# Two layers of cached attention and feed-forward: order of key loads, places of rolled loops, and spare products at the layer border

## The chip, the core and the metric

The kernel runs on one core of one Trainium2 chip. The metric is device time in microseconds (us), the median of several runs. A run's time is a little longer than the span of its instructions in the profile. The engines are TensorE (PE, with its weight loads as PEld), VectorE (DVE), ScalarE (ACT), GpSimd (POOL) and SyncE (SP). SP issues every load here.

## The reference

One step of decoding for a batch of 4, through an attention block, a feed-forward block, and then both once more with the same weights and the same caches. A "layer" below is one pass through attention and feed-forward.

```
attention(x):  q = x @ wq                     # 512 -> 32 heads of 128
               scores = q . k * 128 ** -0.5   # 8 key heads, 4 query heads each, 8192 keys
               o = softmax(scores) @ v
               return concat(o) @ wo
ffn(x):        return (silu(x @ w_gate) * (x @ w_up)) @ w_down      # 512 -> 1792 -> 512
x = x + attention(layernorm(x));  x = x + ffn(layernorm(x))
x = x + attention(layernorm(x));  x = x + ffn(layernorm(x))
```

All inputs are bfloat16. The key and value caches are 4 x 8 x 8192 x 128 each, 64 MB of keys and 64 MB of values, and both layers read them; 273 MB come from memory in one execution.

## The kernel before

**Units.** The work of a layer is cut into 32 units, one for each pair of key head and batch row. A unit has a key block K and a value block V of 2 MB each. Eight slots of 2 MB on the chip hold such blocks (`NSLOT`, tile `kvf`). Layer 0 takes the units in order, 0 to 31. Layer 1 begins with units whose blocks are still on the chip (`kept`), then takes the rest. In this text K29 or V27 is the block of the unit at place 29 or 27 of its layer's order (`unit_order[L]`).

**Order of compute.** `work(L)` (line 320) gives the order in which blocks are computed: K(i), then V(i-1), and so on, with the end K28, V27, K29, V28, K30, K31, V29, V30, V31. `keys` and `values` (542, 568) write the operations of a block out. A key block has eight parts. For each, DVE transposes the keys in place (`turn`, tile `kvf`), and four products on PE add its scores to a bank (`scores`, output `ps<-kvf,zq`). Then a short chain makes the softmax: DVE takes the row maximum (`max_p`, `one<-ps`), PE transposes it and DVE reduces it (`max_t`, `m<-ps`), ACT copies it (`pb<-m`), PE spreads it, ACT scales it (`exps`, `one<-ps,rstd`) and takes the exponentials, DVE transposes the probabilities (`turn_p`, `pT<-pb`), and PE sums them (`total`). A value block is 16 products of 512 columns (`ps<-kvf,pT`), after which ACT and DVE pick out each head's own rows (`own_first`, `own_others`, `acc<-ps,own`). After every fourth unit `out_proj` (648) multiplies with `wo` (`o<-ps`, `ps<-o,wo_sb`). The last two value blocks of a layer use a form with small products (`block_last`, `ps<-pT,kvf`).

**Order of loads.** The list `items` (329) is the order in which SP issues loads. It is the compute order, without the kept blocks, followed by the feed-forward weights of the layer. `pump` issues the next item when its slot is free and stops at the first one whose slot is not. `home` (347) gives each block its slot. In program order a slot is free when its last block is finished; on the chip SP waits on a semaphore for it. SP's queue is in order, so an issue that waits holds back all behind it. The weights of the feed-forward block use slots 6 and 7.

**The layer border.** `center` and `deviation` (675, 693) make the layer norm: DVE sums, a product with ones on PE, and DVE again. `ffn` (743) runs `gate` and `up` (4 x 14 products each, weights `kvf` or, for a part kept from layer 0, `wq_sb`), a chain on DVE and ACT that makes hT, and 14 x 4 products with `w_down` (`ps<-scr,kvf`). While layer 0's `ffn` runs, it already frees places and issues parts of the first keys of layer 1 (`part`). `keep_up3` (727) copies a piece of `w_up` to another place and issues the last of these parts; the copy waits for PE's last read of `wq`. The first two key blocks of layer 1 then hand their slots on in quarters (`quarter`).

**Products that nobody reads.** `warm(n)` (669) makes n products of 128 x 128 with 256 columns from `wq_sb` into the score bank `SBK[1]`. Nothing reads them. Before the change five are made, all at the start of layer 1 (`center(L)`, `warm(L)`, `qrows(..., L)`).

**Rolled loops.** The operations of PE, DVE and ACT are first written to tapes. `roll` (796) finds a stretch of each layer that repeats every four units (`CYCLE`) and plays it as a loop. Where a unit begins on an engine's tape is noted in `heads`; for all three engines this happens in `keys`, when the first block of scores is written (line 546). The loop is opened with

```
with nc.Fori(1, 1 + turns, 1, engines=(only,), head_slot={only: 0}) as i:
```

`head_slot` is the place, counted in instructions, in a block of fetched code at which the loop's first instruction is put; the code ahead of the loop ends with a branch to it. Each product takes two instructions on PE, a weight load and the product.

Of the kernel before, what the change touches and what calls it, by code (L numbers as in the profile page):

```python
# [145 lines left out]
def bass_interleave_layers__gqa_block_cached__swiglu_ffn__decode_kernel(  # L146
# [20 lines left out]
    KT = D // P  # L167
# [16 lines left out]
    NV = NB // 2  # L184
    RUN = 1 << 15
    WIDE = 32
    assert TB == 2 * NA and NV * REP <= QB
    NU = B * G
    scale = float(Dh) ** -0.5
# [2 lines left out]
    with ExitStack() as es:  # L192
# [52 lines left out]
        n = 2 * FO * B  # L245
# [34 lines left out]
        T = _Sync(nc, engines, prog)  # L280
# [48 lines left out]
        items = []  # L329
        for L in range(2):  # L330
            seq = [it for it in work(L) if it not in kept]
            items += seq + [("wg",)] + [("wu",)] * (L == 0) + [("wd",)]
        for n, it in ((3, ("wo", 0)), (6, ("wo", 1)), (9, ("wo", 2)), (12, ("wo", 3))):
            items.insert(n, it)
# [165 lines left out]
        def max_t(u):  # L500
            T.pe(bank(STEP)[0:1, 0:P], mx[:], identf[:], reads=["mx", "ident"], writes=[f"pb{STEP}"],
                 is_transpose=True, start=True, stop=True)
            T.op("dve", lambda e: e.tensor_reduce(m4[:], bank(STEP)[0:1, 0:P].rearrange("p (x h) -> p h x", h=REP),
                                                  AX.X, ALU.max, negate=True),
                 reads=[f"pb{STEP}"], writes=["m4"])
            T.op("act", lambda e: e.activation(mrow.rearrange("p (x h) -> p x h", h=REP),
                                               m4[:].unsqueeze(1).to_broadcast([1, QB, REP]), ACTF.Copy),
                 reads=["m4"], writes=["pb"])
# [33 lines left out]
        def keys(L, u):  # L542
            def block(q):
                first = u == unit_order[L][0]
                if q == 0:
                    for n in T.LATE:
                        heads[n].append(len(T.tape[n]))
                if q == 0 and not first:
                    place_q(u)
                scores(L, u, q)  # L550
                if q == 0 and first:
                    deviation(lsc_sb, "lsc")
                if ("K", L, u) in heirs and (q + 1) % (NB // NQ) == 0 and q < NB - 1:
                    quarter(("K", L, u), q // (NB // NQ))
                if q == NB - 1:
                    finished(("K", L, u))
                    for gap, fn in ((0.0, max_p), (1.0, max_t), (0.9, exps), (1.0, turn_p), (0.3, total)):
                        line.append([gap, u, lambda fn=fn: fn(u)])

            i = unit_order[L].index(u)  # L560
            ahead = unit_order[1][i + 2] if L == 1 and i in (1, 2) else u
            for q in range(NB):
                if (L, ahead, q) not in turned:
                    turn(L, ahead, q)
                blocks.append((0.65, lambda q=q: block(q)))
                drain(LAG)
# [176 lines left out]
        def ffn(last):  # L743
            gb, ub = OBK
            gT = bank(gb)[:, 0:FO * B]
            uT = bank(ub)[:, 0:FO * B]
            fb = lambda ap: ap.rearrange("p (f b) -> p f b", b=B)
            rb = rstd[:].unsqueeze(1).to_broadcast([P, FO, B])
            ks = items[ends[0] + 1:ends[0] + 3]
            n = NB // NQ  # L750
            w6 = KT * F // (TB * Dh) // n * n
            for (w_sb, wname, bk) in (([wg_sb[:, k, :] for k in range(KT)], "wg", gb), (wu_sb, "wu", ub)):
                out = bank(bk)[:, 0:WIDE // B * FO * B].rearrange("p (r f b) -> p f r b", f=FO, b=B)
                for kt in range(KT):
                    if bk == gb and kt == KT // 2:
                        deviation(zero_sb, "zero")
                    for fo in range(FO):
                        f = fo // 2 * 2 * P + fo % 2
                        w = up3(f) if bk == ub and kt == FR and last else w_sb[kt][:, f:f + 2 * P - 1:2]
                        T.pe(out[:, fo, :, :], w, few(xn[:, kt * B:(kt + 1) * B]),  # L760
                             start=(kt + fo == 0), stop=(kt == KT - 1 and fo == FO - 1),
                             reads=["up3"] if bk == ub and kt == FR and last else at_w[wname] + [f"{wname}{kt}", "xn"],
                             writes=[f"pb{bk}"],
                             sig=(fo == FO - 1 and kt == KT - 1))
                if bk == gb and not last:
                    place(ks[0], NKEEP)
                    part(ks[0], NKEEP, 0, w6, sem_p[0])
            T.op("dve", lambda e: e.tensor_tensor(fb(gr), fb(gT), rb, ALU.mult),
                 reads=[f"pb{gb}", "rstd"], writes=["gr"])
            T.op("act", lambda e: e.activation(eg, gr, ACTF.Exp, scale=-1.0), reads=["gr"], writes=["eg"])  # L770
            T.op("dve", lambda e: e.tensor_tensor(fb(gw), fb(gr), rb, ALU.mult), reads=["gr", "rstd"], writes=["gw"])
            T.op("dve", lambda e: e.tensor_scalar(eg, eg, 1.0, None, op0=ALU.add), reads=["eg"], writes=["eg"])
            T.op("dve", lambda e: e.reciprocal(eg, eg), reads=["eg"], writes=["eg"])
            T.op("dve", lambda e: e.tensor_tensor(eg, gw, eg, ALU.mult), reads=["gw", "eg"], writes=["eg"])
            T.op("dve", lambda e: e.tensor_tensor(hT, eg, uT, ALU.mult), reads=[f"pb{ub}", "eg"], writes=["hT"])
            out = bank(OUTB)[:, 0:WIDE // B * XB].rearrange("p (r n b) -> p n r b", n=KT, b=B)
            for fo in range(FO):
                for nt in range(KT):
                    T.pe(out[:, nt, :, :], wd_sb[:, fo, nt * P:(nt + 1) * P], few(hT[:, fo * B:(fo + 1) * B]),
                         start=(fo + nt == 0), stop=(fo == FO - 1 and nt == KT - 1),  # L780
                         reads=["hT"] + at_w["wd", fo // 2], writes=[f"pb{OUTB}"], sig=(nt == KT - 1 and fo % 2 == 1))
                if not last and (f1 - f0 + (fo + 1) * D) % (n * TB * Dh) == 0:
                    i = (f1 - f0 + (fo + 1) * D) // (n * TB * Dh) - NQ
                    if i == 0:
                        part(ks[0], NKEEP, w6, NB, sem_p[1])
                        place(ks[1], NKEEP + 1)
                    else:
                        part(ks[1], NKEEP + 1, (i - 1) * n, i * n, sem_p[1 + i])
            if last:
                T.op("dve", lambda e: e.tensor_tensor(xn[:], xT[:], bank(OUTB)[:, 0:XB], ALU.add),  # L790
                     reads=["x", f"pb{OUTB}"], writes=["xn"])
            else:
                add_to_x()


        def roll(name):
# [18 lines left out]
            for L in range(2):  # L815
                run = {}
                for n in range(L * NU + 1, L * NU + NU - CYCLE - 1):
                    m = n
                    while m + CYCLE < L * NU + NU - 1 and said[m] == said[m + CYCLE] and strides(m) and \
                            strides(m) == strides(n + (m - n) % CYCLE):  # L820
                        m += 1
                    run[n] = m - n
                n = max(run, key=run.get)
                turns = run[n] // CYCLE + 1
                assert turns >= 3
                step = {}
                for k in range(n, n + CYCLE):
                    for key, d in strides(k).items():
                        assert step.setdefault(key, d) == d
                assert step.get(None, 1) == 1  # L830
                T.play(name, ops[at:heads[name][n]])
                with nc.Fori(1, 1 + turns, 1, engines=(only,), head_slot={only: 0}) as i:
                    for k in range(n, n + CYCLE):
                        value = {}
                        for _, _, left, _, _ in part[k]:
                            for sem_, v in left:
                                d = step[id(sem_)]
                                value[id(sem_), v] = engine.to_reg(i * d + (v - d))  # L838
                        T.play(name, part[k], lambda sem_, v: value[id(sem_), v], lambda g: i + (g - 1))
                at = heads[name][n + CYCLE * turns]  # L840
# [13 lines left out]
        for L in range(2):  # L854
# [26 lines left out]
            drain(0.0)  # L881
            flush(line)
            flush(after)
            center()
            ffn(L == 1)

        ob = bank_bf(LNB)
# [38 lines left out]
```

## Time and profile before

| | |
|---|---|
| median of 3 runs | 648.72 us (647.23 to 649.49) |
| the profiled execution, its own time | 649.32 us |
| its span | 647.5 us |
| mean granted clock of TensorE | 0.847 |
| busy: PE, DVE, ACT | 511.1, 446.1, 118.2 us |
| bytes read | 273.42 MB, 422 GB/s over the span |

How to read the rows shown in the prediction. A row of the stretches has the window, its length, the busy time and number of instructions of PE, PEld, DVE, ACT and POOL, the share of its clock that TensorE was granted (1.00 is full), the share of time that the transfer engines were busy, and GB/s. A row of the time order has the start in us, the time it took, engine, line, operation, output and inputs, shapes and the number of instructions merged; in brackets stands how long the engine was idle before it and what it waited for. There "issue" means that the engine waited for nothing that the profile shows. A row of the chain of waits has start, length, what ran, and how many. Since helpers record every operation, nearly all rows have line 99 (PE), 117 (the other engines) or 135 (loads); the tiles tell them apart.

### The profile page before, as it was taken

The numbers are of one execution on the slowest core, as the hardware profiler recorded it, in microseconds if no ns is written. First come the engines' busy times: TensorE is split into PE (matmuls) and PEld (weight loads), VectorE is DVE, ScalarE is ACT, GpSimd is POOL, SyncE is SP. The second block draws the span as 40 slices with busy tenths as digits, with TensorE's granted clock in tenths as the row PEclk, the third lists the DMA queues.
The fourth block names the chain that finished last, engine by engine and source line by source line (L and its number), as shares of the span: only waits on it lengthen the run. The fifth ranks groups of instructions, "written<-read, shape, count | busy, mean of one in ns | idle before, by whom it ended". The sixth has DMA issues, their size and how long they took to land.

```text
span 647.5 us, 12443 instructions
## 1 busy us (share of the span) xinstructions
PE 511.1 (79%) x4901; PEld 328.9 (51%) x4901; DVE 446.1 (69%) x1075; ACT 118.2 (18%) x393; POOL 19.3 (3%) x73
## 2 busy tenths in 40 slices
PE   1757887878878787888887986888888778787886
PEld 1534554545445554554555663555554455454556
DVE  2556576776876767776763745979796777678683
ACT  0011121211221211221221212222121222122121
POOL 0000000000000000000000000000000000000000
PEclk9998687787977879787796997989797978879795
DMA  8999999999999999999999999999999999999995
GB/s 357 434 432 423 431 441 423 437 437 421 442 433 423 441 431 427 442 427 427 441 412 413 393 439 413 417 433 433 427 439 431 427 443 427 431 439 427 424 431 244
DMA packets 12750, 273.83 MB, mean 423 GB/s; under 512 B 3048, under 2 KB 3056, under 8 KB 3056
## 3 DMA queue, kind: packets, MB, share of 16 engines
q1 hardware_dynamic: 12720, 273.44, 98.7%
q8 instruction: 18, 0.29, 0.2%
q14 instruction: 12, 0.10, 0.0%
HBM read 273.42 MB, written 0.00 MB: 422 GB/s over the span
## 4 chain that ended last, share of the span: by engine, by line
DMA 48%; PE 24%; DVE 23%; issue 3%; ACT 1%; SPq 0%; DVEq 0%; POOL 0%; ACTq 0%; POOLq 0%
DMA kvf<-in_A_k_cache_dram 48%; PE ps L99 24%; DVE kvf L117 14%; DVE acc L117 4%; DVE pT L117 1%; DVE one L117 1%; DVE m L117 1%; ACT pb L117 0%; SPq L135 0%; DVE scr L117 0%; ACT acc L117 0%; DVE oT L117 0%; DVEq L838 0%; DVE o L117 0%; DVE xn L117 0%
## 5 line engine op out<-in xcount | busy, mean ns | idle before, releaser
L117 DVE STREAM_TRANSPOSE kvf<-kvf 128x512 f32<-128x512 f32 x488 | 322.3, 686 | 72.2 <-DMA kvf<-in_A_k_cache_dram 72.2
L99 PE MATMUL ps<-kvf,zq 128*128 128x256 bf16 x2048 | 334.6, 308 | 19.1 <-DVE kvf L117 12.0
L99 PEld LDWEIGHTS ps<-kvf,zq 128*128 128x128 bf16 x2048 | 205.7, 112 | 89.9 <-DVE kvf L117 35.7
L117 ACT ACTIVATE pb<-m 1x128 f32<-1x128 f32 x64 | 19.7, 308 | 439.7 <-DVE m L117 439.7
L99 PE MATMUL ps<-kvf,pT 128*16 128x512 bf16 x960 | 69.8, 415 | 2.0 <-DVE rl L117 2.0
L117 DVE SCALAR_TENSOR_TENSOR acc<-ps,own,acc 128x128 f32<-128x128 f32 x180 | 63.1, 351 | 7.4 <-ACT acc L117 2.7
L117 DVE TENSOR_REDUCE one<-ps 128x1 f32<-128x256 f32 x64 | 25.8, 404 | 34.9 <-PE ps L99 34.5
L99 PE MATMUL ps<-identf,one 128*1 128x128 f32 x64 | 18.0, 282 | 39.2 <-DVE one L117 39.0
L99 PE MATMUL ps<-head,acc 128*128 128x4 f32 x120 | 24.7, 276 | 20.1 <-DVE acc L117 19.9
L99 PEld LDWEIGHTS ps<-identf,one 128*1 128x1 f32 x64 | 5.2, 80 | 69.2 <-DVE one L117 62.3
L99 PEld LDWEIGHTS ps<-head,acc 128*128 128x128 f32 x120 | 20.5, 214 | 36.4 <-DVE acc L117 35.3
L99 PEld LDWEIGHTS ps<-kvf,pT 128*16 128x16 bf16 x960 | 19.4, 92 | 35.6 <-issue 24.6
L99 PE MATMUL ps<-o,wo_sb 128*128 128x32 bf16 x256 | 26.8, 186 | 13.2 <-DVE o L117 13.2
L117 ACT ACTIVATE pb<-ps,one,rstd 128x256 bf16<-128x256 f32 x64 | 36.0, 563 | 2.1
L482 POOL TENSOR_TENSOR zq<-scr,quad 128x64 bf16<-128x64 bf16 x62 | 18.1, 292 | 603.5 <-PE ps L99 564.3
L99 PE MATMUL ps<-one,pb 1*128 1x1 f32 x128 | 26.4, 273 | 11.3 <-ACT pb L117 11.2
L99 PEld LDWEIGHTS ps<-one,pb 1*128 1x128 f32 x128 | 21.0, 204 | 28.3 <-ACT pb L117 24.9
L117 DVE STREAM_TRANSPOSE pT<-pb 128x256 bf16<-128x256 bf16 x64 | 26.0, 407 | 8.0 <-ACT pb L117 7.9
L99 PEld LDWEIGHTS ps<-o,wo_sb 128*128 (+1 forms) x256 | 22.7, 103 | 16.9 <-issue 9.3
L99 PEld LDWEIGHTS ps<-rsm,one 128*128 128x128 f32 x128 | 24.5, 237 | 8.3 <-ACT rsm L117 6.4
L99 PE MATMUL ps<-rsm,one 128*128 128x4 f32 x128 | 21.9, 242 | 5.2 <-ACT rsm L117 5.2
L117 DVE TENSOR_TENSOR xT<-xT,ps 128x16 f32<-128x16 f32 x17 | 2.9, 171 | 31.5 <-PE ps L99 31.5
(64 smaller groups left out, 202.2 us busy)
## 6 DMA issues: line engine op xcount, KB each, us to landing
kvf<-in_A_k_cache_dram SPq DMA_DIRECT2D x56, 2048.0 KB, 29.0
kvf<-in_A_v_cache_dram SPq DMA_DIRECT2D x56, 2048.0 KB, 32.6
kvf<-in_A_k_cache_dram SPq DMA_DIRECT2D x20, 512.0 KB, 7.4
kvf<-in_A_v_cache_dram SPq DMA_DIRECT2D x20, 512.0 KB, 10.8
wq_sb<-in_A_wq_dram SPq DMA_DIRECT2D x4, 1024.0 KB, 7.7
wo_sb<-in_A_wo_dram SPq DMA_DIRECT2D x8, 512.0 KB, 37.8
kvf<-in_B_w_gate_dram SPq DMA_DIRECT2D x8, 448.0 KB, 15.8
kvf<-in_B_w_down_dram SPq DMA_DIRECT2D x14, 256.0 KB, 16.9
```

The lines of the kernel that those rows point to most:

```text
L99: return e.matmul(out, lhsT=lhsT if at is None else lhsT(place(at)), rhs=rhs, **kw)
L117: self.tape[engname].append((repr((name, args, kw)), lambda e, _: getattr(e, name)(*args, **kw), left, sig, None))
L482: T.op(eng, lambda e: e.tensor_tensor(dst, q4, m4_, ALU.mult), reads=keys_ + ["quad"], writes=["zq"])
```

## The change

Five edits, in three groups.

```diff
         for L in range(2):
             seq = [it for it in work(L) if it not in kept]
+            for k, v in ((29, 27), (30, 28)):
+
+                it = ("K", L, unit_order[L][k])
+                seq.remove(it)
+                seq.insert(seq.index(("V", L, unit_order[L][v])), it)
             items += seq + [("wg",)] + [("wu",)] * (L == 0) + [("wd",)]
```

The end of each layer's list of loads was K28, V27, K29, V28, K30, K31, V29, V30, V31. It becomes K28, K29, V27, K30, V28, K31, V29, V30, V31. The order of compute stays.

```diff
+    HEADS = (0, 100)
...
-                    for n in T.LATE:
+                    for n in ("pe", "dve"):
                         heads[n].append(len(T.tape[n]))
...
+            heads["act"].append(len(T.tape["act"]))
             T.op("act", lambda e: e.activation(mrow.rearrange("p (x h) -> p x h", h=REP),
...
-                with nc.Fori(1, 1 + turns, 1, engines=(only,), head_slot={only: 0}) as i:
+                with nc.Fori(1, 1 + turns, 1, engines=(only,), head_slot={only: HEADS[L] if name == "pe" else 0}) as i:
```

ACT's units now begin at the copy of the maximum in `max_t`, so its loops begin there too. PE's loop in layer 1 is put at slot 100 instead of 0; in layer 0 it stays at 0.

```diff
+                    if bk == ub and kt == KT - 1 and not last:
+                        warm(1)
                     for fo in range(FO):
...
             for fo in range(FO):
+                if not last:
+                    warm(1 + (fo == 0) if fo % 2 == 0 else 0)
                 for nt in range(KT):
...
-            center()
+            center(1 - L)
             ffn(L == 1)
```

At the border between the layers twelve products more are made that nobody reads: in `center` after layer 0's attention two before the product with ones and one behind it; in layer 0's `up` one ahead of the last 14 products; in layer 0's `w_down` loop two before the first group of four products and one before every second group after it (six). Layer 1's end gets none.

## The prediction

> **What bounds the kernel now.** I read the page's slices and chain first, then the stretches where the transfers fall off, then what each engine waited for there, and last the time order of the two layer ends.
>
> ```profile
> DMA  8999999999999999999999999999999999999995
> DMA 48%; PE 24%; DVE 23%; issue 3%; ACT 1%; SPq 0%; DVEq 0%; POOL 0%; ACTq 0%; POOLq 0%
> 500.00:600.00 100.00, 79.48 (x652) 48.51 (x647) 75.09 (x176) 19.47 (x66) 3.22 (x11) 0.88 1.00 433
> 350.00:355.00 5.00, 4.74 (x50) 3.20 (x51) 3.04 (x10) 2.33 (x4) 0.00 (x0) 0.50 1.00 406
> 355.00:360.00 5.00, 4.50 (x31) 3.21 (x29) 1.26 (x3) 0.02 (x1) 0.29 (x1) 0.75 0.96 334
> 360.00:365.00 5.00, 5.00 (x51) 3.33 (x49) 4.69 (x11) 1.52 (x5) 0.29 (x1) 1.00 0.98 397
> 395.00:400.00 5.00, 3.55 (x32) 2.73 (x33) 2.08 (x6) 1.12 (x4) 0.00 (x0) 0.50 0.97 411
> 400.00:405.00 5.00, 4.55 (x39) 2.28 (x37) 3.99 (x9) 1.77 (x6) 0.29 (x1) 0.82 0.96 393
> 405.00:410.00 5.00, 4.70 (x48) 2.77 (x45) 4.95 (x13) 0.08 (x1) 0.29 (x1) 1.00 1.00 406
> 640.00:645.00 5.00, 3.96 (x135) 3.66 (x132) 1.73 (x7) 0.63 (x3) 0.00 (x0) 0.50 0.19 77
> ```
>
> The transfers fill nearly every slice, at 433 GB/s where nothing disturbs them (500 to 600 us). So time is to be had in three places only. **Border**, 350 to 365 us: 406, 334 and 397 instead of 433, (27 + 99 + 36) x 5 / 433 = 1.9 us lost. **Dip**, 395 to 410 us: (22 + 40 + 27) x 5 / 433 = 1.0 us. **Tail**: transfers fade after 640 us and the span lasts to 647.5. A wait anywhere else is covered by loads already queued.
>
> The sum is made against the profiled execution, 649.32 us (span 647.5 and 1.82 around it). It lies 0.6 above the median of 648.72, so I take the change in us from the one and put it on the other. A measurement of this kernel can tell about 0.3% (1.9 us) from no change.
>
> **ScalarE's loop starts elsewhere.** The head of its repeated block moves from the first score block of a unit to the copy of the maximum in `max_t`.
>
> ```profile
> ACT one L117 <- issue: 11.4, 2, 5.9
> 46.09 0.26 ACT L117 ACTIVATE one<-ps,rstd 128x1 f32<-128x1 f32 x1 [5.88 <-issue]
> 36.07 37.20 DMA kvf<-in_A_k_cache_dram
> 388.84 0.31 ACT L117 ACTIVATE pb<-m 1x128 f32<-1x128 f32 x1 [5.25 <-DVE m L117]
> 394.91 0.26 ACT L117 ACTIVATE one<-ps,rstd 128x1 f32<-128x1 f32 x1 [5.51 <-issue]
> 396.45 0.61 PE L99 MATMUL ps<-o,wo_sb 128*128 128x32 bf16 x16 [4.17 <-DVE o L117]
> 400.81 0.47 SPq L135 DMA_DIRECT2D kvf<-in_A_k_cache_dram  x1
> ```
>
> Twice, once for each layer, ScalarE stood 5.9 and 5.5 us with nothing to wait for, between two steps of one softmax: its instructions were not there. Behind it in layer 1 waited exp, DVE's turn of the probabilities, the cast of o, PE (4.17 us), and so the keys' load at 400.81: that is the dip. In layer 0 the load issued at 36.07 landed 37 us later, so the queue was deep and that stall cost nothing. The edit removes no instruction; the fetch now comes ahead of the copy of the maximum, which waits 5.25 us for DVE anyway. Of 5.51 that leaves 0.3 bare. Value -1.0, the whole dip, since keys that load 5 us sooner outrun a loss of 1.0; ends 0 (the loads come no sooner) and -1.0.
>
> **Keys before values.** For the units 29 and 30 of each layer's order K is issued before V27 and V28; SP issues the same loads, none added. Each moves past one load of 2 MB, 2.1 / 433 = 4.85 us.
>
> ```profile
> 564.84 0.47 SPq L135 DMA_DIRECT2D kvf<-in_A_v_cache_dram  x1
> 577.61 0.47 SPq L135 DMA_DIRECT2D kvf<-in_A_k_cache_dram  x1
> 577.61 26.55 DMA kvf<-in_A_k_cache_dram
> 603.51 1.04 PE L99 MATMUL ps<-kvf,pT 128*16 128x512 bf16 x16
> 605.26 0.27 PE L99 MATMUL ps<-identf,one 128*1 128x128 f32 x1 [0.71 <-DVE one L117]
> 604.18 0.71 DVE L117 STREAM_TRANSPOSE kvf<-kvf 128x512 f32<-128x512 f32 x1 [2.71 <-DMA kvf<-in_A_k_cache_dram]
> 606.34 0.24 DVE L117 TENSOR_REDUCE m<-ps 1x4 f32<-1x128 f32 x1
> 610.72 5.59 PE ps L99 x34
> ```
>
> On SP, K29 waits until 577.61 for its slot, and V27 (issued at 564.84) now queues behind it, 13 us later. That starves nothing: a load issued at 577.61 lands 26.55 later, so some 26 us, less the 4.85 of V27, are ahead of it. K29 lands at 599.3 and V27 at 604.2, the places exchanged. DVE then need not stand 2.71 us for K29: its first transpose and the maximum of the unit before run early. But PE's V27 products, at 603.51 now, wait until 604.2 (0.7), and the maximum's transpose stands behind them at 605.3, as before. DVE reads it at 605.5 instead of 606.34, because its two queued key transposes are done. So the late one becomes V27, and the gain is 0.8 and not 4.85. From 610.72 to the end PE and DVE hand on to each other without waiting for a load, so it is carried. Value -0.7; ends 0 (V27 waits a whole load) and -1.6 (the floor below). At the end of layer 0 the same gain runs into the border.
>
> **PE's block in layer 1 starts at slot 100.** Both programs' loops hold the same instructions; what moves is where PE's code crosses from one fetched block to the next after the loop: 100 slots sooner, 50 products (a load and a product each).
>
> ```profile
> 633.56 1.86 PE ps L99 x64
> 638.47 3.44 PE ps L99 x109
> 641.91 0.47 issue
> 642.38 0.31 PE ps L99 x5
> 642.99 1.69 PE ps L99 x56
> kvf<-in_B_w_down_dram SPq DMA_DIRECT2D x2, 256.0 KB, 16.8
> 625.39 3.39 SPq L135 DMA_DIRECT2D kvf<-in_B_w_down_dram  x2
> ```
>
> PE stops 0.47 us at 641.91, five products short of the end of `up`. That crossing moves to 55 products short, 50 x 3.44 / 109 = 1.6 us sooner; the crossing before it also moves 50 products, 50 x 1.86 / 64 = 1.5 us sooner, and with it the fetch. So fetch and need move together, and the 0.47 may go. Value -0.4; ends -0.5 (gone) and +1.1 (the fetch comes no sooner: it ends at 642.38 and 50 products still follow). **Floor:** the last of `w_down`, issued some 0.6 after 625.39, lands 16.8 later, at 642.8; the last eight products behind it (8/56 x 1.69 = 0.2) end at 643.1, where 644.7 stands now. The tail can give 1.6, and I take 1.1 of it.
>
> The Trainium skill ("Runtime: NRT & Kernel Launch", section "Instruction fetch mechanics") calls the crossing of a block mostly hidden. By that this term is nil and the sum 0.4 smaller; the 0.47 here, and the 2.93 below, speak against it.
>
> **Products that nobody reads.** `center` of layer 0 gets 3, `up` 1, `w_down` 8: twelve, on PE alone.
>
> ```profile
> 342.94 12.09 SPq L135 DMA_DIRECT2D kvf<-in_A_k_cache_dram  x8
> 347.17 0.29 PE L99 MATMUL ps<-xn,kvf 128*128 128x32 bf16 x5 [2.93 <-issue]
> 347.77 1.67 PE L99 MATMUL ps<-scr,kvf 128*128 128x32 bf16 x56 [0.31 <-DVE scr L117]
> 349.28 0.59 PE L99 MATMUL ps<-wq_sb 128*128 128x256 bf16 x2
> L99 PE MATMUL ps<-wq_sb 128*128 128x256 bf16 x5 | 1.7, 388 | 0.0
> 352.46 6.25 PE ps L99 x34
> 384.59 2.38 PE L99 MATMUL ps<-kvf,zq 128*128 128x256 bf16 x20
> 347.20:350.60 3.40, 3.04 (x66) 2.31 (x65) 0.61 (x4) 0.00 (x0) 0.00 (x0) 0.51 1.02 422
> ```
>
> Two that exist take 0.59 together and one 0.39, so 0.2 is added by each. The 3 and the 1 and the first 2 of `w_down` stand before waits of 0.3 to 0.5 us (for DVE's sums, the `up` weights, hT): hidden. The other 6, 1.2 us, lie between `w_down` products that PE now runs without a stop, since the 2.93 us at the fetch has let the weights land. Nothing in the change shortens that fetch: its crossing only moves four products forward. Behind PE wait SP's loads into the places that `w_down` frees, and the first keys' scores of layer 1. Those scores run at half clock now (6.25 us for 34, 184 ns; 119 ns at full), and a fuller stretch from 347.2 could lift it. The 0.7 from the earlier keys and 32 x 0.065 = 2.1 from a raised clock stand against 1.2 of products. The border's transfers cannot give more than 1.9. Value 0, between -1.9 (the stop vanishes too, or the clock rises) and +4.7 (12 x 0.388, all in the way).
>
> The Trainium skill ("TensorE: Matmul & The Clock Gate", section "What's actually happening") has the clock rise after one busy window of about 3.4 us. By that the filled stretch would lift it before the scores, and the sum would be 1.9 larger: the first rival. That 3.04 of 3.40 us busy were not enough here leaves it open.
>
> **Sum:** -1.0 - 0.7 - 0.4 + 0 = -2.1, 647.2 for the profiled execution, 646.6 for the median.
>
> **Rivals.** (1) *The border gains too.* The products hold the clock, the first scores end 2 us sooner, and SP refills before the queue runs dry: -2.1 - 1.9 = -4.0, 644.7. For it: 334 GB/s in 355:360 with PE busy at half clock. Against: the 2.93 us stop, which these products do not touch. Chance 0.22.
> (2) *Only the end moves.* The dip stays because ScalarE's fetch, wherever it stands, is not covered (5.25 us of wait against 5.51, and PE's half clock behind it), and the border takes what layer 0 gained: -1.1, 647.6. For it: the transfers fill all slices. Against: the load at 400.81 hangs on that very stall. Chance 0.25.
> (3) *Slower: the products stand in the way.* Place: the `w_down` loop of layer 0. It decides if they run after the weights have landed and the clock stays low: then up to 12 x 0.388 = 4.7 us come ahead of the first keys' scores, and SP's loads start as much later, in a stretch whose queue is already near empty. 4.7 - 2.1 = +2.6, 651.3. For it: the fetch stop, which makes PE the late one. Against: half of the twelve have a wait to lie in. Chance 0.12.
> (4) *No effect of the reordering* as V27 is waited for instead, and the fetch in the tail lands in a worse place (+1.1): about -1.0 + 1.1 = 0, 648.8. Chance 0.06.
> The forecast has 0.35.
>
> **Numbers.** Forecast 646.6, its own range +-0.9 from the two tail terms. Faster by over 0.3% (under 646.8) are (1) and some 0.28 of the forecast's 0.35: 0.50. Within are (2), (4) and the forecast's rest: 0.38. Slower: (3), 0.12. The range goes from a little under (1), 644.2, to 649.6, between (4) and (3).
>
> **What would show it.** ScalarE: no 5.5 us "issue" row near 390, PE's 4.17 for o gone, 433 GB/s in 400:410. Keys: DVE's 2.71 near 604 gone, out_proj's products some 0.7 sooner against the transfers. Slot 100: no "issue" row in `up` of layer 1. Border: the 2.93 row still there, the products of `w_down` taking 2.9 instead of 1.7 us, and the GB/s of 355:365 telling (1) from (3). The forecast is wrong if the dip stays, or if transfers in 350:365 fall well below 334.

## The result and the profile after
| | before | after |
|---|---|---|
| median | 649.01 us (647.23 to 651.4, 20 runs) | 647.11 us (646.37 to 648.24, 20 runs) |
| the profiled execution, its own time | 649.32 us | 646.91 us |
| its span | 647.5 us | 645.1 us |
| mean granted clock of TensorE | 0.847 | 0.862 |

The ratio of after to before is 0.9967, with a 95% interval of 0.9959 to 0.9975: 0.33% faster, some 2.1 us, where 2.1 had been forecast (647.2 for the profiled execution).

The stretches of the kernel after, with the columns of the prediction's rows (window, length, busy time of PE, PEld, DVE, ACT and POOL, granted clock, share of the transfers, GB/s):

```profile
350.00:355.00 5.00, 4.40 (x51) 2.97 (x51) 3.25 (x12) 2.16 (x4) 0.00 (x0) 0.66 0.98 416
355.00:360.00 5.00, 4.50 (x40) 3.46 (x39) 2.43 (x6) 0.50 (x2) 0.29 (x1) 1.00 0.91 331
360.00:365.00 5.00, 4.82 (x48) 3.15 (x47) 4.72 (x11) 1.75 (x6) 0.29 (x1) 1.00 1.00 406
395.00:400.00 5.00, 5.00 (x35) 2.45 (x34) 2.80 (x7) 0.07 (x1) 0.29 (x1) 0.58 0.98 419
400.00:405.00 5.00, 4.24 (x35) 2.80 (x32) 4.85 (x12) 1.70 (x6) 0.00 (x0) 1.00 1.03 437
405.00:410.00 5.00, 4.34 (x45) 2.74 (x43) 4.88 (x13) 1.77 (x6) 0.29 (x1) 1.00 1.01 434
640.00:645.00 5.00, 2.41 (x75) 2.01 (x71) 1.22 (x5) 0.00 (x0) 0.00 (x0) 0.84 0.11 43
```

The dip is gone: 419, 437 and 434 GB/s stand where 411, 393 and 406 stood. The border is as it was: 416, 331 and 406 against 406, 334 and 397. The tail has shrunk.

At the dip, first ACT's row in the table of waits (us in total, times, longest), then ACT's and PE's rows in time order around layer 1's loop head:

```profile
ACT pb L117 <- issue: 5.7, 1, 5.7
```

```profile
389.29 0.31 ACT L117 ACTIVATE pb<-m 1x128 f32<-1x128 f32 x1 [6.86 <-DVE m L117]
389.50 0.34 ACT L117 ACTIVATE acc<-ps,own 128x128 f32<-128x128 f32 x1
390.06 0.26 ACT L117 ACTIVATE one<-ps,rstd 128x1 f32<-128x1 f32 x1 [0.22 <-PE ps L99]
393.32 0.61 PE L99 MATMUL ps<-o,wo_sb 128*128 128x32 bf16 x16 [0.58 <-DVE o L117]
```

One such stop is left, layer 0's. In layer 1 the copy of the maximum now begins the loop; ACT waits 6.86 us for DVE there anyway, and whatever the fetch takes lies inside that wait. The scaling follows the copy by 0.77 us (389.29 to 390.06), not by 6.07 (388.84 to 394.91), and PE waits 0.58 us for o instead of 4.17.

The late loads, in time order (SP's issue of V27, then PE and DVE):

```profile
577.69 0.59 SPq L135 DMA_DIRECT2D kvf<-in_A_v_cache_dram  x1
603.98 1.04 PE L99 MATMUL ps<-kvf,pT 128*16 128x512 bf16 x16 [0.40 <-DMA kvf<-in_A_v_cache_dram]
605.25 0.28 DVE L117 TENSOR_REDUCE m<-ps 1x4 f32<-1x128 f32 x1
```

V27 has become the late block, as forecast: it lands 26.2 us after its issue, at 603.9 (604.2 forecast). From the landing to DVE's maximum it is now 605.25 - 603.9 = 1.3 us; before, from K29's landing at 604.16 (577.61 + 26.55), it was 606.34 - 604.16 = 2.2. In the traces of the experiments below it is 2.2 wherever the order of loads is the old one (five traces, with before) and 1.3 to 1.5 wherever it is the new one (nine, with this).

The chain of waits in the tail, and then the end of `up` in time order:

```profile
609.68 5.16 PE ps L99 x34
...
632.08 1.77 PE ps L99 x64
...
640.84 1.63 PE ps L99 x56
```

```profile
639.87 0.54 PE L99 MATMUL ps<-xn,wq_sb 128*128 128x32 bf16 x14
```

No row of "issue" splits the 14 products of `up`, where 9 and 5 stood around 0.47 us. The 2.4 us of span, set against the rows of before, divide into four: up to 609.68 1.04 (stream and keys), from there to 632.08 0.44 (the 34 products took 5.16 instead of 5.59, at a granted clock of 0.67 instead of 0.50), to 640.84 0.67 (the stop of 0.47 among it), and 0.25 behind, most of it the clock too.

The border, in time order and then from the chain:

```profile
344.60 0.56 PE L99 MATMUL ps<-xn,kvf 128*128 128x32 bf16 x14 [0.30 <-DMA kvf<-in_B_w_up_dram]
...
348.94 0.36 PE L99 MATMUL ps<-scr,kvf 128*128 128x32 bf16 x8 [0.69 <-DMA kvf<-in_B_w_down_dram]
```

```profile
335.15 14.29 DMA kvf<-in_B_w_down_dram
...
349.48 0.38 PE ps L99 x8
...
352.62 4.92 PE ps L99 x34
```

This is not what was forecast. The 2.93 us stop is gone, the landings of `w_down` pace the products (the last at 335.15 + 14.29 = 349.44), and the spare products lie in those waits. The last eight products end at 349.86, 0.40 later than before (347.77 + 1.67 = 349.44), and the first scores of layer 1 begin at 352.62 instead of 352.46: the border as a whole stayed where it was.

### The profile page after: what moved, and what is told of

The parts are those of the page before. It is cut to its first block, busy times and chain, and to the rows that moved or that the text cites. A ratio compares the mean times of both kernels' runs of the same rounds, so it can differ in the third digit from the quotient of the medians.

```text
span 645.1 us, 12463 instructions
## 1 busy us (share of the span) xinstructions
PE 509.1 (79%) x4913; PEld 327.5 (51%) x4913; DVE 445.6 (69%) x1075; ACT 118.3 (18%) x393; POOL 19.3 (3%) x73
## 4 chain that ended last, share of the span: by engine, by line
DMA 53%; DVE 21%; PE 21%; SPq 3%; issue 2%; ACT 1%; DVEq 0%; POOL 0%; POOLq 0%
DMA kvf<-in_A_k_cache_dram 47%; PE ps L99 21%; DVE kvf L117 13%; DMA kvf<-in_A_v_cache_dram 4%; DVE acc L117 4%; SPq L135 3%; DMA kvf<-in_B_w_down_dram 2%; DVE one L117 1%; DVE pT L117 1%; DVE m L117 1%; DVE scr L117 0%; ACT pb L117 0%; DVEq L849 0%; DVE oT L117 0%; ACT acc L117 0%
## 5 line engine op out<-in xcount | busy, mean ns | idle before, releaser
L99 PE MATMUL ps<-kvf,pT 128*16 128x512 bf16 x960 | 67.1, 402 | 2.0 <-DVE rl L117 1.2
```

Source lines behind the costliest of these rows:

```text
L99: return e.matmul(out, lhsT=lhsT if at is None else lhsT(place(at)), rhs=rhs, **kw)
```

## The experiments
Two theories stood at the start. **A**: three of the parts (ScalarE's loop head, keys, slot) each take a piece, and the spare products do nothing. **B**: the spare products do part of it, since the border's stop is gone where they run. The first four kernels are the kernel before with one part alone, the next four the whole change with one part left out.

**Keys alone.**
```diff
+            for k, v in ((29, 27), (30, 28)):
+                it = ("K", L, unit_order[L][k])
+                seq.remove(it)
+                seq.insert(seq.index(("V", L, unit_order[L][v])), it)
```


> The kernel before with the new order of loads alone. Theory A (each of three edits gives its own share, in its own place): K29 lands some 4.85 us before V27, the first transpose of K29 no longer waits 2.7 us, the products of wo that follow come about 0.7 us sooner against the loads, and the time falls by 0.7 to 1.1 us (0.11 to 0.17%). The 5.5 us issue row of ScalarE in layer 1 and the 393 GB/s of 400 to 405 us stay. Theory B (the gain is the border's: the spare products remove PE's 2.93 us stop at the fetch): no gain here, within 0.3 us.

Ratio 0.9990 (0.9977 to 1.0003). **ScalarE's loop head alone.**
```diff
-                    for n in T.LATE:
+                    for n in ("pe", "dve"):
...
+            heads["act"].append(len(T.tape["act"]))
```


> The kernel before with ScalarE's loop head moved alone. Theory A: the 5.5 us issue row in layer 1 goes into the wait for DVE's maximum, the stretch 400 to 405 us has over 425 GB/s, and the time falls by 0.5 to 1.0 us. Theory B: no gain, within 0.3 us; the loads are covered anyway. The issue row of layer 0 stays 5 to 6 us long in both.

Ratio 0.9990 (0.9981 to 0.9999). **Slot 100 alone.**
```diff
+    HEADS = (0, 100)
...
+                with nc.Fori(1, 1 + turns, 1, engines=(only,), head_slot={only: HEADS[L] if name == "pe" else 0}) as i:
```


> The kernel before with PE's loop of layer 1 at slot 100 alone. Theory A: no issue row in up of layer 1 (0.47 before), the end 0.4 to 0.6 us sooner. Theory B: no change, within 0.3 us. A third way: the fetch lands in a worse place, and the time grows by up to 1.1 us.

Ratio 0.9992 (0.9983 to 1.0002). **The spare products alone.**
```diff
+                    if bk == ub and kt == KT - 1 and not last:
+                        warm(1)
...
+                if not last:
+                    warm(1 + (fo == 0) if fo % 2 == 0 else 0)
...
-            center()
+            center(1 - L)
```


> The kernel before with the twelve products alone. Theory A: within 0.4 us of before, on either side; what PE gains at the fetch, if anything, the last weights of w_down take back. Theory B: the 2.93 us issue row at the border is gone or under 1 us, the loads in 350 to 365 us recover, and the time falls by 1 to 2 us. The slower rival of the prediction: the products stand in the way and the time grows by over 1 us.

Ratio 1.0005 (0.9993 to 1.0017). Each of the first three gives about 0.1%, too little to tell from nothing in two of the three; the products give nothing. The next four leave one part of the whole change out.

**Without the spare products.**
```diff
-                    if bk == ub and kt == KT - 1 and not last:
-                        warm(1)
...
-                if not last:
-                    warm(1 + (fo == 0) if fo % 2 == 0 else 0)
...
-            center(1 - L)
+            center()
```


> The changed kernel without the twelve products: keys, ScalarE's loop head and slot 100 together. Theory A (three shares that add, the products worth nothing): a ratio of 0.996 to 0.998 to before, as the whole change has (0.9967), no 5.5 us row of ScalarE in layer 1. Theory B (the products carry the gain): 0.999 to 1.000. A third way, from the products alone, which measured 1.0005: they cost a little, and this is the fastest of all, 0.996 or under.

Ratio 0.9969 (0.9957 to 0.9982), which is that of the whole change. In its time order the stop at the border is back, and costs nothing:

```profile
345.98 0.29 PE L99 MATMUL ps<-xn,kvf 128*128 128x32 bf16 x5 [1.70 <-issue]
346.58 1.46 PE L99 MATMUL ps<-scr,kvf 128*128 128x32 bf16 x48 [0.31 <-DVE scr L117]
349.20 0.40 PE L99 MATMUL ps<-scr,kvf 128*128 128x32 bf16 x8 [1.16 <-DMA kvf<-in_B_w_down_dram]
```

PE stands 1.70 us for nothing that the profile shows, catches up with 48 products, and then waits 1.16 us for the last landing: the end is at 349.60, 0.26 before that of the whole change. Theory B falls.

**Without the earlier keys.**
```diff
-            for k, v in ((29, 27), (30, 28)):
...
-                seq.insert(seq.index(("V", L, unit_order[L][v])), it)
```


> The changed kernel with the old order of loads. Theory A: K29's first transpose waits 2.7 us again near 604, and the time is 0.5 to 1.0 us longer than with the whole change, a ratio of 0.9975 to 0.9985. Rival (the keys' share is the noise of its own run): 0.9967 stays.

Ratio 0.9989 (0.9979 to 0.9998). Here the stop at the border was long in the profiled execution, as its time order and the chain show:

```profile
346.45 0.40 PE L99 MATMUL ps<-xn,kvf 128*128 128x32 bf16 x9 [2.21 <-issue]
```

```profile
346.45 3.67 PE ps L99 x73
```

The 73 products are 9 of `up`, the 56 of `w_down` and 8 spare ones, run without a wait to 350.12. The last weights, issued at 334.9, had landed 13.3 us later, at 348.3. So behind a long stop the spare products do stand in the way: without them the last eight, some 0.4 behind that landing, could have ended at 348.7, up to 1.4 sooner (an estimate).

**Without ScalarE's loop head.**
```diff
-            heads["act"].append(len(T.tape["act"]))
...
-                    for n in ("pe", "dve"):
+                    for n in T.LATE:
```


> The changed kernel with ScalarE's loop head where it was. Theory A: the issue row of 5 to 6 us in layer 1 is back, the stretch 400 to 410 us falls under 410 GB/s, the last loads land about 0.5 to 1 us later, and the ratio is 0.9977 to 0.9985. Rival (the loads are covered, the dip costs nothing in the end): 0.9967 stays.

Ratio 0.9985 (0.9971 to 1.0). ACT's stop and PE's wait for the last weights are both in its time order:

```profile
395.20 0.26 ACT L117 ACTIVATE one<-ps,rstd 128x1 f32<-128x1 f32 x1 [5.78 <-issue]
643.84 0.40 PE L99 MATMUL ps<-scr,kvf 128*128 128x32 bf16 x8 [0.23 <-DMA kvf<-in_B_w_down_dram]
```

In this execution the floor decides: the last of `w_down` lands only at 643.8, and the end waits for it. Whether the transfers end too late in every execution without ScalarE's part, one trace does not show.

**Without slot 100.**
```diff
-                with nc.Fori(1, 1 + turns, 1, engines=(only,), head_slot={only: HEADS[L] if name == "pe" else 0}) as i:
+                with nc.Fori(1, 1 + turns, 1, engines=(only,), head_slot={only: 0}) as i:
```


> The changed kernel with PE's loop of layer 1 at slot 0. Theory A: an issue row of 0.4 to 1.0 us is back in up of layer 1, and the ratio is 0.9973 to 0.9980. Rival: without the five products behind the crossing the end is set by the last weights of w_down, and 0.9967 stays.

Ratio 0.9989 (0.9980 to 0.9998). Taken out of the whole (0.9967), ScalarE's part is worth 0.18%, keys and slot 0.22% each, the products 0.02%; alone the three summed to 0.28%. Theory A stands as far as the places go: keys and slot, left out, come clear of the interval of the whole (0.9959 to 0.9975), and ScalarE's part nearly does. The sizes as measured do not add: left out they sum to 0.62%, alone to 0.28%, and the whole is worth 0.33%. With intervals of 0.1% and more each, it stays open whether the parts help one another.

Three more kernels tried the parts further. **14 more spare products.**
```diff
-                    warm(1 + (fo == 0) if fo % 2 == 0 else 0)
+                    warm(3 + (fo == 0) if fo % 2 == 0 else 0)
```


> The whole change with three spare products instead of one before every second group of layer 0's w_down (14 more, 26 in all). Theory: these products lie in waits for the landings of w_down, so the border's transfers stay as they are and the time stays within 0.15% of the whole change, 647.0 to 648.0; the windows of 350:365 carry no less than before. Rival (the slower case of the prediction): PE is the late one there, and 14 products of 0.2 to 0.39 us come ahead of the first scores of layer 1: 2.7 to 5.4 us more, 649.8 to 652.5.

Ratio 0.9985 (0.9975 to 0.9996): between the two, some 0.18% or 1.2 us over the whole change, from two groups of runs whose intervals just touch. The chain of waits of its one profiled execution:

```profile
345.19 5.47 PE ps L99 x92
...
353.41 3.88 PE ps L99 x34
```

Now PE is the late one at the border: `w_down` runs without a wait to 345.19 + 5.47 = 350.66, 0.80 later than in the whole change, not 2.7 to 5.4. The first scores begin 0.79 later and, at full clock, take 1.04 less. They end at 357.29 against 357.54, so this one trace does not show where 1.2 us went.

**Slot 232.**
```diff
-    HEADS = (0, 100)
+    HEADS = (0, 232)
```


> The whole change with layer 1's loop of PE at slot 232 instead of 100, so that the crossing into the next block of code falls a few products into the last w_down instead of at the head of the last up. Theory: what slot 100 gave is that the crossing falls where PE waits or the code is there already; at 232 an issue row of 0.3 to 1.0 us comes back near the last w_down, and the time is some 0.5 us over the whole change, 647.6, like the kernel that leaves slot 100 out (648.4) or a little better. Rival: the place does not matter, the last landing of w_down sets the end, and the time is that of the whole change, 647.1.

Ratio 0.9985 (0.9976 to 0.9993), 648.27 us. The chain of its tail, where slot 0 (products alone) is set beside it in a second fence:

```profile
632.83 1.79 PE ps L99 x64
634.87 0.44 PE ps L99 x16
635.56 0.50 PE ps L99 x12
636.07 0.37 issue
636.44 0.30 PE ps L99 x4
...
642.16 1.69 PE ps L99 x56
```

```profile
634.51 1.88 PE ps L99 x64
...
639.44 3.44 PE ps L99 x109
642.88 1.02 issue
643.90 0.31 PE ps L99 x5
644.51 1.69 PE ps L99 x56
```

The stop follows the slot, but to another place than I had expected: four products before the end of `out_proj`, and not in `w_down`. 232 slots are 116 products, so the crossing lies 116 + 5 = 121 before the end of `up`; the 112 products of `gate` and `up`, 4 with ones and 4 of `out_proj` are 120.

**Keys and ScalarE's loop head together.** The diff is the first two above, both at once.

> Earlier keys and ScalarE's loop head together, without slot 100 and without spare products. Theory: the two need each other (each alone gave 0.10%, each taken out of the whole cost 0.16 to 0.22%): the stream runs on at the loop head, and with it the last values, which the earlier keys had made the late ones, come sooner; together they give 0.2% or more, 647.9 or less. Rival: each part gives its own 0.1% and the rest comes from slot 100: 648.1 or more.

Ratio 0.9985 (0.9974 to 0.9996), by time neither more nor less than the sum of the two alone: 0.15% against 0.20%. That the two need each other is not shown.

**The whole change once more**, with nothing edited but an empty line.

> The whole change again, in a comparison of its own. If ratios of separate comparisons can be set side by side, it comes out between 0.996 and 0.9975, and the 0.9985 of the kernels with 14 more products and with slot 232 means that these edits give back half of the gain. If it comes out at 0.998 to 0.999, the comparisons differ by as much as the edits do, and the shares of the single edits cannot be told apart in time. The stop of PE ahead of the last products of layer 0's up, 2.93 before the change and none after it, comes out between none and 2.9 us whatever the code.

Ratio 0.9970 (0.9958 to 0.9982) against 0.9967: by this one repeat, groups of runs can be set side by side. The next table does that for the traces. Its columns are the time ratio, GB/s in 395 to 410 us, DVE's maximum before the last `out_proj` but one (`m<-ps`, 606.34 before), the time from the 64 small value products to the first `w_down` product in the tail (633.56 to 642.99 before), PE's "issue" stop in `up` at the border, and GB/s in 350 to 365 us.

| kernel | ratio | 395:410 | max, us | tail, us | stop, us | 350:365 |
|---|---|---|---|---|---|---|
| before | 1 | 404 | 606.34 | 9.43 | 2.93 | 379 |
| keys | 0.9990 | 403 | 607.31 | 8.86 | 0.92 | 385 |
| slot | 0.9992 | 388 | 607.31 | 8.87 | 1.39 | 371 |
| products | 1.0005 | 387 | 607.27 | 10.00 | 0.47 | 389 |
| without ScalarE's | 0.9985 | 417 | 605.70 | 9.03 | 1.25 | 360 |
| ScalarE's | 0.9990 | 418 | 604.98 | 9.23 | 0.30 | 397 |
| without keys | 0.9989 | 429 | 605.73 | 8.84 | 2.21 | 369 |
| without slot | 0.9989 | 430 | 604.80 | 9.11 | 0 | 374 |
| keys, ScalarE's | 0.9985 | 429 | 604.89 | 9.04 | 0 | 371 |
| slot 232 | 0.9985 | 426 | 604.97 | 9.33 | 1.09 | 380 |
| without products | 0.9969 | 425 | 604.75 | 8.83 | 1.70 | 381 |
| 14 more | 0.9985 | 425 | 605.51 | 8.75 | 0 | 380 |
| whole | 0.9967 | 430 | 605.25 | 8.76 | 0 | 385 |
| whole again | 0.9970 | 437 | 605.18 | 8.86 | 0 | 391 |

One execution of each is little, but groups of them tell. The first five rows lack ScalarE's edit: their mean in 395 to 410 is 400 GB/s (387 to 417), that of the other nine 428 (418 to 437), so the edit brings 28 x 15 / 433 = 0.97 us of stream. DVE's maximum stands at 606.8 and 605.1 in the mean, 1.7 sooner; the traces do not place the part of it that the dip leaves over. The tail takes 8.75 to 9.03 us in the seven kernels with slot 100 (mean 8.85), 8.86 to 10.00 in the six with slot 0 (mean 9.28), and 9.33 with slot 232.
## Why the prediction was right, and where it was not
**ScalarE's loop head (-1.0): right, mechanism and size.** The stop of 4.9 to 5.8 us is in all five kernels without the edit and in none of the nine with it, and the dip gave 0.97 us of stream. By time the part is worth 0.10% alone and 0.18% in the whole, 0.6 to 1.2 us. That a fetch "wherever it stands, is not covered" (second rival) is refuted by 390.06: 6.86 us of waiting for DVE covered it. Set against before's own trace the gain looks smaller at 606 us than against the rest, since that was earlier than most without the edit (606.34 against 607.3 in three others; the fourth, without ScalarE's part but with the rest, had 605.70).

**Keys before values (-0.7): right in mechanism, the size between 0.3 and 1.4.** V27 is late in place of K29, for the reason given. From the late landing to DVE's maximum 2.2 us became 1.3, which is 0.9, and the two groups of traces do not overlap. But the maximum itself, with ScalarE's part in place, stands at 605.05 in the mean of seven traces with the keys moved and at 605.36 in the two without, since V27 lands a little later than K29 did (603.7 against 603.2 in the mean of the same traces). By time the part is worth 0.1% alone and 0.22% in the whole, 0.6 to 1.4 us, with intervals that hold 0.7.

**Slot 100 (-0.4): right in size, the reason in part open.** No stop in `up` in seven kernels of seven, 0.43 us less tail in the mean. Slot 232, where a stop of 0.37 comes back in `out_proj` and the tail takes 9.33, shows that the place is what counts and not the change of it. Why the crossing is free at slot 100 the traces do not show: 55 products before the end of `up` PE runs on without a wait to hide it in, and with slot 0 the crossing five products before the end was free once too (keys alone). In time the part is worth 0.08% to 0.22%. The Trainium skill ("Runtime: NRT & Kernel Launch", section "Instruction fetch mechanics") calls a crossing mostly hidden; with slot 0 this kernel's traces show 0.47, 0.45, 1.02, 0.34, 0.17 and none at one and the same crossing, so it can be anything between hidden and 1 us.

**Twelve spare products (0): right in the number, wrong in its reason.** The step that failed is "Nothing in the change shortens that fetch", and with it that six products, 1.2 us, lie between `w_down` products "that PE now runs without a stop". The 2.93 us was one execution's value and no property of the code: with slot 100 alone PE's program is the same up to layer 1's loop, and the stop was 1.39; with and without the products it came out between none and 2.21 us in 13 other traces. Where it is short, PE reaches `w_down` before its weights, and the products lie in the waits for them (0.69 in the whole change); the last landing, at 348.3 to 349.4 us, set the end of `w_down` in ten of the 14 traces, with the products or without. Where it was long, 2.21 and 1.25 with the products in, the mechanism was the one forecast and PE was late. So the 1.2 us of products is a price that an execution pays or not, and in the median it cannot be told from nothing (1.0005 alone, 0.02% in the whole). The slower rival (651.3) had the right place and too high a price: 14 more products moved the end of `w_down` by 0.80.

**The border's gain (first rival, 644.7): did not come.** The clock did rise in the whole change: the first scores took 4.92 and 5.36 us in its two executions, 5.59 without the products, 6.25 before. The products are not shown to be the cause: 5.13 was measured with ScalarE's part alone, which has none of them, and 6.54 with the products alone. In the whole change the scores ended 0.9 to 1.2 us sooner than before, and the transfers gained nothing by it. In 350 to 365 us the mean is 378 GB/s over the eight kernels with products and 381 over the six without.

**The sum.** -2.1 forecast, -2.4 in the profiled span, -1.9 between the medians, -2.1 by the ratio. That these lie so close is in part luck. The forecast median of 646.6 started from 648.72, three runs; twenty gave 649.01, and 647.11 behind the change. The parts of the span fall otherwise than forecast: 1.04 came before 609.68, where -1.0 and -0.7 stood, and 0.67 in place of 0.4 around the stop. The other 0.7 came from the clock in the tail, which the sum did not have and which changes from one execution to the next: the 34 products took 5.16 here, 5.59 before, and 5.09 to 5.61 in eleven other traces.
## What to carry to other kernels
A loop head is a place where an engine may stand 5 us for its code; put it where that engine waits for another anyway, and look at what load hangs behind it. Shifting a loop's slot moves the crossings behind it; judge a place over several traces, for a stop at a crossing is a different number each time. Before a stop in one trace is charged to an edit, ask what would set the end without it: here it was the landing of the last weights.
## What the runs showed of the hardware
**A crossing's price is not the code's.** The one in `up` at the border cost PE 0 to 2.93 us in 14 traces, and 2.93, 0.92, 1.39, 0.30 and 0 in the five (before, keys, slot, ScalarE's, keys and ScalarE's) in which PE's own work at the border is the same.

**In these traces TensorE's clock rises behind a stretch that is all but full.** One-microsecond stretches with 14 more products:

```profile
346.00:347.00 1.00, 1.00 (x13) 0.79 (x12) 0.00 (x1) 0.00 (x0) 0.00 (x0) 0.50 1.14 459
347.00:348.00 1.00, 1.00 (x14) 0.78 (x12) 0.00 (x0) 0.00 (x0) 0.00 (x0) 0.50 0.92 385
348.00:349.00 1.00, 1.00 (x22) 0.89 (x21) 0.00 (x0) 0.00 (x0) 0.00 (x0) 0.78 1.17 483
349.00:350.00 1.00, 1.00 (x26) 0.92 (x23) 0.00 (x0) 0.00 (x0) 0.00 (x0) 1.00 0.96 393
```

and with slot 232:

```profile
348.00:349.00 1.00, 0.94 (x15) 0.36 (x12) 0.00 (x0) 0.00 (x0) 0.00 (x0) 0.50 1.18 500
350.00:351.00 1.00, 0.89 (x10) 0.59 (x11) 0.45 (x4) 0.00 (x0) 0.00 (x0) 0.50 1.15 475
...
356.00:357.00 1.00, 1.00 (x7) 0.70 (x5) 0.00 (x0) 0.00 (x0) 0.00 (x0) 0.50 0.97 377
357.00:358.00 1.00, 1.00 (x8) 0.72 (x7) 0.00 (x0) 0.00 (x0) 0.00 (x0) 0.66 0.65 262
```

In the first, PE is busy without a gap from 345.19, and the granted clock doubles within 348 to 349, some 3.3 us later (0.78 is 0.44 us of half clock and 0.56 of full). In the second it is 0.89 to 1.00 busy in every such stretch from 346 to 357 and stays at half clock to 357; PE is busy without a gap there from 352.4, and the clock doubles only at some 357.7 (0.66), 5.3 us later. The Trainium skill ("TensorE: Matmul & The Clock Gate", section "What's actually happening") gives one busy window of about 3.4 us; the first trace agrees; in the second the rise took longer, and its stretches of nine tenths busy did not count as one.
